# A tuned attention-and-MLP kernel: the first batch's second half is up-projected in seven products of quarters of 192 tokens

## The chip, the cores and the metric

The kernel runs on one core of a Trainium2 chip. The metric is the time of one execution on the device in microseconds. A core has a matrix engine (TensorE, in the profile PE, with PEld for its weight loads), VectorE (DVE), ScalarE (ACT), GpSimd (POOL), and SyncE (SP), which here only issues transfers. Each engine works through its own queue in order, and engines wait for one another by semaphores. TensorE writes its results to PSUM, from where VectorE or ScalarE takes them to the on-chip memory (SBUF).

## What is computed

Attention in which a query sees the keys of its own cluster only, then two matrix products with g = h - tanh(h) between them. Shapes: q, k, v (4 batches, 8 heads, 768 tokens, 64), centroids (8, 16, 64), w_in (512, 2048), w_out (2048, 512), all 32-bit floats in the kernel.

```python
q_assign = np.argmax(np.einsum('bhsd,hcd->bhsc', q_n, c_n), axis=-1)
k_assign = np.argmax(np.einsum('bhsd,hcd->bhsc', k_n, c_n), axis=-1)
mask = q_assign[:, :, :, None] == k_assign[:, :, None, :]
scores = np.where(mask, scale * np.matmul(q, k.transpose(0, 1, 3, 2)), -1000000000.0)
...
x = np.ascontiguousarray(attn_out.transpose(0, 2, 1, 3)).reshape(B * S, H * D)
h = x @ w_in
g = h - np.tanh(h)
return (g @ w_out).astype(np.float32)
```

## The kernel before

**Steps.** Attention is done for pairs of heads, four pairs a batch, and for a half of 384 query tokens at a time. One step of the outer loop (`for at, (n, half, s) in enumerate(steps)`) does a third of the keys for one pair and one half. The first batch does its first half for all four pairs (steps 0 to 11), then its second half (12 to 23); later batches take both halves of a pair together, 24 steps a batch. In each step TensorE gets the scores of the next step (`begin`, L451), and the products with the values (`value`, L505); ScalarE takes the exponentials (L473), VectorE selects by cluster code (`select`, L483), and GpSimd adds up the denominators (L496). After the last step of a pair the result lies in `xT[n][:, half]`, and a while later it is multiplied by the reciprocal of its denominator (`divide`, `scale`).

**The matrix products lag by one stage.** They are lists of items with a cost in planner's units, and each step takes the items that keep pace with an even share of the list. The first batch's first half is worked off in steps 12 to 23, its second half in steps 24 to 47, batches 1 and 2 in steps 48 to 71 and 72 to 95, and batch 3 at the end. An item calls `between()` once or twice, and each call emits a share of the step's other work (`todo`): selects first, then the stages of the next pairs' routing, then denominators, then weights to be rounded or factors to be made. So the order on every engine's queue follows from this list.

**Two forms of the products.** The first batch uses `plain_items`: 16 blocks of 128 of the 2048 inner columns, for each four chunks of 128 rows of w_in times 384 tokens (L676, tile `h`), tanh on ScalarE (L681) and the subtraction on VectorE (L683), then the products with w_out (L692, tile `o`). Later batches use `strassen_items`: inner columns, tokens and model columns are each cut in two, and seven products of quarters replace eight. Their left factors are sums of quarters of w_in and w_out, made once (`up_maker`, `down_maker`, L773), stored to device memory (L737, L756) and streamed back, one stream for each pair of blocks (`fetch_factors`, L795; tile `stream`, three buffers). Their right factors are differences of quarters of the attention output (`right_factors`, L832). `up_product` (L871, tile `pu`) does one of the seven, and each result is added on VectorE from PSUM (L859) or copied by ScalarE (L876); `shrink` then takes tanh (L864) and subtracts on GpSimd (L866). With three PSUM buffers (`ps_f`, shared by all small products), the fourth product from any one waits for nothing but the first's add.

**Memory.** The pool `first` holds what only the first batch needs (weights w_out, the tiles of g, rounding buffers `rawp`, and two pairs' transposed q and k in `turnp0`), `first_in` holds w_in. `open_stream` gives up w_in for the streams at step 39 and `open_late` gives up the rest at step 48. The factor sums use the three buffers of `rawp`, in which weights are rounded up to step 20. In steps 24 to 46, ten steps that are not at certain places in a pair (`light`) get a share of the makers' list.

Of the kernel before, what the change touches and what calls it, by code (L numbers as in the profile page):

```python
# [30 lines left out]
F32 = mybir.dt.float32  # L31
# [4 lines left out]
ALU = mybir.AluOpType  # L36
# [3 lines left out]
P = 128  # L40
# [18 lines left out]
def kernel(  # L59
# [119 lines left out]
    def fast():  # L179
# [439 lines left out]
        def spread_out(n: int, half: int):  # L619
            back = lists.pop((n, half))  # L620
            if joined(n):
                pool = late_pools.get("den", sump)
                dens[n, 1] = pool.tile([P, TB], F32, name="den")
                for i in range(2):
                    for h in range(2):
                        nc.sync.dma_start(
                            dens[n, i][h * D : h * D + D], back[i, h : h + 1].to_broadcast([D, TB])
                        )
                return
            for h in range(2):  # L630
# [34 lines left out]
        def plain_items(half: int):  # L665
# [39 lines left out]
            if half == 0:  # L705

                order = [(s, i) for i in range(NQ4) for s in range(2)] + order[2 * NQ4 :]
            return [(2.6, 1, lambda between, f=f: up(f, between)) for f in sequence] + [
                (3.4, 1, lambda between, s=s, i=i: project(s, i, between)) for s, i in order
            ]  # L710

# [74 lines left out]
        def fetch_factors(n: int):  # L786

            if n < (B - 1) * PER:
                i = n % PER
                t = streams[n] = late_pools["stream"].tile([P, HF, HM], F32, name="stream")  # L790
                if i < HF:
                    t = streams[n] = t.rearrange("p a b -> p (a b)")[:, 0 : 7 * CH * P].rearrange(
                        "p (c k f) -> p c k f", k=7, c=CH
                    )
                nc.sync.dma_start(t, up_factors[i] if i < HF else down_factors[i - HF])  # L795

        late_pools, diffs = {}, {}

        def open_stream():
            first_in.close()  # L800
            late_pools["stream"] = cx.enter_context(
                tc.tile_pool(name="stream_late", bufs=3, side="right", reuse_waits="tile")
            )
            late_pools["den"] = cx.enter_context(
                tc.tile_pool(name="den_late", bufs=1, side="right", reuse_waits="tile")
            )
            for n in range(2):
                fetch_factors(n)

        def open_late():  # L810
            first.close()
            for name, bufs in (
                ("diff", 1), ("u", 2), ("s", 2), ("th", 2), ("g", 1), ("left", 1), ("du", 1),
                ("c", 4), ("raw", 2),
            ):
# [4 lines left out]
            late_pools["S1"] = late_pools["left"].tile([P, HF, TB], F32, name="S1")  # L820

        def right_factors(b: int, c: int):

            if c == 0:
                diffs[b] = late_pools["diff"].tile([P, 3, CH, TB], F32, name="diff")
            d = diffs[b]
            x, y = xT[b * HP + c], xT[b * HP + CH + c]
# [6 lines left out]
        def strassen_items(b: int):  # L834
            base = (b - 1) * PER

            held = {}
            G, left1 = late_pools["G"], late_pools["S1"]

            def up_product(i: int, k_: int, between):  # L840
                which = PRODUCTS[k_]
                x = [xT[b * HP + c] for c in range(CD)]
                d = diffs[b]
                right = {
                    1: [x[c][:, 0] for c in range(CH)], 2: [x[CH + c][:, 0] for c in range(CH)],
                    3: [x[CH + c][:, 1] for c in range(CH)], 4: [d[:, 2, c] for c in range(CH)],
                    5: [d[:, 0, c] for c in range(CH)], 6: [d[:, 1, c] for c in range(CH)],
                    7: [x[c][:, 1] for c in range(CH)],
                }[which]
                if k_ == 0:  # L850
                    held[i] = (
                        late_pools["s"].tile([P, TB], F32, name="s"),
                        late_pools["u"].tile([P, 2, TB], F32, name="u"),
                    )
                s, u = held[i]
                g = G[:, i]

                def add(out, x, y):
                    nc.vector.tensor_tensor(out=out, in0=x, in1=y, op=ALU.add)  # L859

                def shrink(f: int, halves_=slice(0, 2)):
                    t = g[:, f, halves_]
                    th = late_pools["th"].tile([P, 2, TB], F32, name="th")[:, halves_]
                    nc.scalar.activation(out=th, in_=t, func=ACT.Tanh)  # L864
                    t, th = (x.rearrange("p a n -> p (a n)") for x in (t, th))
                    nc.gpsimd.tensor_tensor(out=t, in0=t, in1=th, op=ALU.subtract)  # L866

                ps = ps_f.tile([P, TB], F32, name="pu", tag="f")
                for c in range(CH):
                    for r in halves:  # L870
                        nc.tensor.matmul(  # L871
# [3 lines left out]
                if which == 1:  # L875
                    nc.scalar.copy(out=s, in_=ps)  # L876
                elif which == 2:
                    add(g[:, 0, 0], ps, s)
                    if i == HF - 1:
                        shrink(0, slice(0, 1))  # L880
                elif which == 6:
                    fetch_factors(base + i + 2)
                    add(u[:, 0], ps, s)
                elif which == 7:
                    add(u[:, 1], ps, u[:, 0])
                elif which == 4:
                    add(g[:, 1, 0], ps, u[:, 1])
                elif which == 5:
                    add(u[:, 0], ps, u[:, 0])
                    add(g[:, 1, 1], ps, u[:, 1])  # L890
                    shrink(1)
                else:
                    add(g[:, 0, 1], ps, u[:, 0])

                    shrink(0, slice(1 if i == HF - 1 else 0, 2))
                between()
                if k_ == len(PRODUCTS) - 1:

                    nc.gpsimd.tensor_tensor(out=left1[:, i], in0=g[:, 0, 1], in1=g[:, 1, 1], op=ALU.add)
                    nc.gpsimd.tensor_tensor(  # L900
                        out=g[:, 0, 1], in0=g[:, 0, 0], in1=g[:, 0, 1], op=ALU.subtract
                    )
                    streams.pop(base + i)

            us = {}

            def down_product(k_: int, j: int, between):
# [49 lines left out]
                between()  # L957


            return [  # L960
                (1.3, 1, lambda between, i=i, k_=k_: up_product(i, k_, between))
                for i in range(HF) for k_ in range(len(PRODUCTS))
            ] + [
                (3.4, 2, lambda between, k_=k_, j=j: down_product(k_, j, between))
                for k_ in range(len(PRODUCTS)) for j in range(HCH)
            ]
# [136 lines left out]
        for at, (n, half, s) in enumerate(steps):  # L1103
            b, p = pairs[n]
            following = steps[at + 1] if at + 1 < len(steps) else None
            if at == 4 * HALF:
                open_late()
            if at == 4 * HALF - 9:
                open_stream()
            if at in fills:  # L1110
                fill, over = fills[at][0](), fills[at][1]
                whole, spent, since = sum(it[0] for it in fill), 0.0, at
            if at == 2 * HALF:
                makers = [it for i in range(2) for it in up_maker(i)]
                makers += [it for i in range(2) for it in down_maker(i)]
            now = []
            part = (at - since + 1) / over
            while fill and (spent + fill[0][0] / 2 <= whole * part or part == 1):
# [86 lines left out]
            listed = []  # L1205

            light = [i for i in range(at, 4 * HALF - 2) if i % 3 and i % 6 != 1]
            if makers and at in light:
                share = -(-len(makers) // len(light))
                todo += makers[:share]  # L1210
                del makers[:share]
# [24 lines left out]
            it()  # L1236
        right_factors(B - 1, CH - 1)
        tail = strassen_items(B - 1)

        PRS = len(PRODUCTS)  # L1240
        tail = tail[:2] + tail[PRS : PRS + 2] + tail[2:PRS] + tail[PRS + 2 :]
        for it in tail[:2]:
            it[2](lambda: None)

# [215 lines left out]
```

## Time and profile before

Median of three runs: 982.78 us (982.29 to 982.94). The profiled execution has a span of 981.3 us.

| engine | busy, us | instructions |
|---|---|---|
| TensorE, matmuls | 972.3 | 6456 |
| TensorE, weight loads | 461.1 | 6456 |
| VectorE | 534.5 | 1010 |
| ScalarE | 316.6 | 484 |
| GpSimd | 498.8 | 347 |

Where the stages lie, by the chain of waits: up-products of the first half start at 79.8 us, its projection at 142.4, the up-products of the second half at 205.9, its projection at 290.1, the later batches' up-products at 374.7, 607.5 and 830.3. The first batch's steps 20, 21, 22 and 23 begin their scores at 159.9, 170.3, 180.5 and 190.3 us.

How to read it: a group's line gives line of code, engine, operation, output and inputs, shapes and count; behind the bar the busy time in us and the mean of one in ns; behind the next the idle time before them and what ended it. The chain of waits is followed back from the last instruction; its pieces in order of time have start, length, what, and the number of instructions. A window's line gives each engine's busy time in a stretch, the clock as a share of full speed, the share of the transfer engines' time and the GB/s. Matmuls overlap at their ends, so their busy times are a little longer than their spacing.

### The profile page before, as it was taken

The page shows a single profiled execution, that of the slowest core. Times are in us where ns is not written, and L with a number is a line of the kernel's source. Part 1 is how long each engine was busy: PE and PEld are TensorE (multiplying, and loading weights), DVE is VectorE, ACT ScalarE, POOL GpSimd, SP SyncE. Part 2 cuts the span into 40 slices and gives each one's busy share as a digit, 9 for nine tenths or more (in the row PEclk, how much of TensorE's full clock was granted, in tenths as well). Part 3 has the DMA queues.
Part 4 walks back from the last instruction along what each step waited for, and adds up shares of the span by engine and source line. Part 5 has one row for each costly group of instructions (what it writes and reads, how often), then busy time and mean ns, then how long its engine had stood idle before and what let it go on. Part 6 is the DMA issues. An engine that isn't in the chain of part 4 may idle for free.

```text
span 981.3 us, 16550 instructions
## 1 busy us (share of the span) xinstructions
PE 972.3 (99%) x6456; PEld 461.1 (47%) x6456; DVE 534.5 (54%) x1010; ACT 316.6 (32%) x484; POOL 498.8 (51%) x347
## 2 busy tenths in 40 slices
PE   9999999999999999999999999999999999999997
PEld 5433443344443334444455555444455555444664
DVE  6458656447566577647655457655754436543011
ACT  5586554233332333233422222333242121222000
POOL 1026334445445454677686345666688445466600
PEclk9999999999999999999999999999999999999999
DMA  7664452024665633463544646345343132233221
GB/s 201 185 192 142 147 143 94 30 73 132 156 204 166 173 116 110 148 195 99 186 151 158 189 136 201 110 151 149 123 159 135 62 118 95 83 113 129 104 103 35
DMA packets 113385, 132.47 MB, mean 135 GB/s; under 512 B 60388, under 2 KB 93076, under 8 KB 110612
## 3 DMA queue, kind: packets, MB, share of 16 engines
q1 hardware_dynamic: 106916, 109.81, 36.5%
q0 software_dynamic: 6240, 21.50, 6.3%
q8 instruction: 53, 0.87, 0.4%
q14 instruction: 32, 0.26, 0.1%
q10 hardware_dynamic: 144, 0.03, 0.0%
HBM read 110.14 MB, written 21.17 MB: 134 GB/s over the span
## 4 chain that ended last, share of the span: by engine, by line
PE 97%; DVE 1%; DMA 0%; issue 0%; SPq 0%; ACT 0%; DVEq 0%
PE pd L922 22%; PE pu L871 22%; PE sc L451 14%; PE av L505 14%; PE o L692 8%; PE h L676 8%; PE pt L332 2%; PE sim L351 1%; PE den L520 1%; PE warm L302 1%; PE den L566 1%; PE den L539 1%; PE pr L364 1%; DVE e L483 1%; DMA row<-q_codes 0%; PE pq L396 0%
## 5 line engine op out<-in xcount | busy, mean ns | idle before, releaser
L496 POOL TENSOR_TENSOR sum<-sum,e 128x768 f32<-128x768 f32 x112 | 207.2, 1850 | 98.0 <-DVE e L483 92.1
L483 DVE SCALAR_TENSOR_TENSOR e<-row,code,sc 128x384 f32<-128x384 bf16 x336 | 186.2, 607 | 104.2 <-ACT sc L473 89.9
L473 ACT ACTIVATE sc<-sc 128x768 f32<-128x768 f32 x168 | 125.9, 792 | 215.8 <-PE sc L451 206.4
L922 PE MATMUL pd<-stream,G 128*64 128x256 f32 x1728 | 191.5, 379 | 0.0
L922 PEld LDWEIGHTS pd<-stream,G 128*64 128x64 f32 x1728 | 123.7, 137 | 67.0 <-issue 7.7
L451 PE MATMUL sc<-t,t 64*128 64x384 f32 x768 | 150.2, 509 | 0.4 <-ACT e L473 0.3
L505 PE MATMUL av<-e,vals 128*64 128x384 f32 x768 | 145.6, 498 | 0.4 <-DVE e L483 0.4
L871 PE MATMUL pu<-xT,stream 128*64 128x384 f32 x768 | 134.9, 488 | 0.7 <-DVE top L372 0.7
L866 POOL TENSOR_TENSOR G<-G,th 128x768 f32<-128x768 f32 (+1 forms) x51 | 87.3, 1723 | 93.9 <-ACT th L864 93.9
L871 PE MATMUL pu<-diff,stream 128*64 128x384 f32 x576 | 102.3, 488 | 0.0
L451 PEld LDWEIGHTS sc<-t,t 64*128 64x128 f32 x768 | 65.8, 186 | 75.0 <-issue 40.8
L492 POOL TENSOR_TENSOR sum<-e 128x768 f32<-128x768 f32 x28 | 55.5, 1983 | 77.9 <-DVE e L483 42.2
L871 PEld LDWEIGHTS pu<-xT,stream 128*64 128x64 f32 x768 | 54.1, 137 | 69.6 <-issue 61.9
L864 ACT ACTIVATE th<-G 128x768 f32<-128x768 f32 (+1 forms) x51 | 40.9, 806 | 141.2 <-DVE G L859 141.2
L692 PE MATMUL o<-w_out,g 128*64 128x512 f32 x384 | 86.4, 594 | 0.0
L505 PEld LDWEIGHTS av<-e,vals 128*64 128x64 f32 x768 | 47.5, 136 | 82.5 <-issue 79.7
L676 PE MATMUL h<-xT,w_in 128*64 128x384 f32 x512 | 86.3, 487 | 0.0
L871 PEld LDWEIGHTS pu<-diff,stream 128*64 128x64 f32 x576 | 40.4, 137 | 51.0 <-issue 44.7
L859 DVE TENSOR_TENSOR G<-pu,u 128x384 f32<-128x384 f32 x72 | 39.8, 553 | 43.5 <-PE pu L871 43.5
L676 PEld LDWEIGHTS h<-xT,w_in 128*64 128x64 f32 x512 | 36.4, 137 | 46.2 <-issue 45.1
L933 DVE SCALAR_TENSOR_TENSOR c<-pd,du 128x256 f32<-128x256 f32 x36 | 15.2, 421 | 67.0 <-PE pd L922 67.0
L692 PEld LDWEIGHTS o<-w_out,g 128*64 128x64 f32 x384 | 27.0, 137 | 50.1 <-issue 49.4
(131 smaller groups left out, 828.9 us busy)
## 6 DMA issues: line engine op xcount, KB each, us to landing
stream<-up_factors SPq DMA_DIRECT2D x24, 896.0 KB
stream<-down_factors SPq DMA_DIRECT2D x21, 1024.0 KB
raw<-in_moe_w_in_dram POOLq DMA_DIRECT2D x16, 512.0 KB, 4.7
raw<-in_moe_w_out_dram POOLq DMA_DIRECT2D x16, 512.0 KB, 3.9
again<-in_moe_w_in_dram SPq DMA_DIRECT2D x32, 256.0 KB
again<-in_moe_w_out_dram SPq DMA_DIRECT2D x32, 256.0 KB
x<-in_q_dram SPq DMA_DIRECT2D x32, 192.0 KB
x<-in_k_dram SPq DMA_DIRECT2D x32, 192.0 KB
```

The source lines that it names most:

```text
L451: nc.tensor.matmul(sc[i][:, h, 0:TB], lhsT=turned[n, 1][r].rearrange("p a n -> p (a n)")[:, j * P : (j + 1) * P], rhs=turned[n, 0][r, half ...
L473: nc.scalar.activation(out=out, in_=sc[i][:, :, 0:TB], func=ACT.Exp, scale=SCALE)
L483: nc.vector.scalar_tensor_tensor(out=e[:, h], in0=rows[n, half][:, h], scalar=codes[n][:, 1, j // HCH, h, j % HCH : j % HCH + 1], in1=sc[: ...
L492: nc.gpsimd.tensor_tensor(out=s, in0=pair[0], in1=pair[1], op=ALU.add)
L496: nc.gpsimd.tensor_tensor(out=s, in0=s, in1=pair[i], op=ALU.add)
L505: nc.tensor.matmul(avs[n, half][h * D : h * D + D], lhsT=vals[n][:, h, j], rhs=e[i][:, h], start=(j == 0), stop=(j == NCH - 1),)
L676: nc.tensor.matmul(h[r], lhsT=w_in[i][:, c, o * P : (o + 1) * P][:, r], rhs=xT[c][:, half], start=(c == 0), stop=(c == CD - 1),)
L692: nc.tensor.matmul(acc[sub][r], lhsT=gs[f % HF][:, f // HF, sub * P : (sub + 1) * P][:, r], rhs=w_out[f // FQ][:, f % FQ], start=(f == seq ...
L864: nc.scalar.activation(out=th, in_=t, func=ACT.Tanh)
L866: nc.gpsimd.tensor_tensor(out=t, in0=t, in1=th, op=ALU.subtract)
L871: nc.tensor.matmul(ps[r], lhsT=streams[base + i][:, c, k_, r], rhs=right[c], start=(c == 0), stop=(c == CH - 1),)
L922: nc.tensor.matmul(ps[r], lhsT=left(i)[:, r], rhs=t[:, i], start=(i == 0), stop=(i == HF - 1))
```

## The change

The up-projection of the first batch's second half takes the seven-product form, with its 384 tokens cut into two quarters of 192. It replaces 16 blocks of plain products by 8 x 7 products of half the rows, to do an eighth less multiplication. For this the up factors have to exist earlier: they are made in steps 20 to 22, at the end of the first half's stage, the space of w_in is given up at step 23, and the first two streams are fetched there. The up factors are then streamed once more than before (eight more streams). The projection of that half stays as it was.

The seven-product code becomes `up_items`, shared by both uses, with functions for where a quarter of g lies, how it is shrunk, and what follows a finished block. Tiles for the first batch's use come from pools that live at that time: partial sums in `turnp0`, right factors in a pool of their own. The late buffer for denominators moves: before step 48 it is now a tile of `turnp0`. The order that starts two blocks' first two products ahead of the third, until now only at the end of the kernel, is a function used twice.

```diff
@@ plain_items
-            return [(2.6, 1, lambda between, f=f: up(f, between)) for f in sequence] + [
+            ups = [(2.6, 1, lambda between, f=f: up(f, between)) for f in sequence]
+            if half == 1:
+                ups = half_up_items(gs)
+            return ups + [
                 (3.4, 1, lambda between, s=s, i=i: project(s, i, between)) for s, i in order
@@ spread_out
-                pool = late_pools.get("den", sump)
-                dens[n, 1] = pool.tile([P, TB], F32, name="den")
+                if "den" in late_pools:
+                    dens[n, 1] = late_pools["den"].tile([P, TB], F32, name="den")
+                else:
+                    dens[n, 1] = turnp0.tile([P, 2, TB], F32, name="t0")[:, 0]
@@ fetch_factors, open_stream
-                i = n % PER
+                i = n + HF if n < 0 else n % PER
...
+            half_pools["diff"] = mid.enter_context(
+                tc.tile_pool(name="diff_mid", bufs=1, side="right", reuse_waits="tile")
             )
             for n in range(2):
-                fetch_factors(n)
+                fetch_factors(n - HF)
@@ up_items (from strassen_items)
+            width = TB if b else TB // 2
...
-                ps = ps_f.tile([P, TB], F32, name="pu", tag="f")
+                ps = ps_f.tile([P, TB], F32, name="pu", tag="f")[:, 0:width]
...
+        def start_without(items):
+            n = len(PRODUCTS)
+            return items[:2] + items[n : n + 2] + items[2:n] + items[n + 2 :]
...
+            def shrink(i: int, f: int, parts):
+                cols = slice(parts.start * W, parts.stop * W)
+                t = gs[i][:, f, cols]
+                th = thp.tile([P, TB], F32, name="th")[:, cols]
+                nc.scalar.activation(out=th, in_=t, func=ACT.Tanh)
+                nc.gpsimd.tensor_tensor(out=t, in0=t, in1=th, op=ALU.subtract)
+
+            return start_without(up_items(0, -HF, quarter, shrink, lambda i: None))
@@ the loop over steps
-            if at == 4 * HALF - 9:
+            if at == 2 * HALF - 1:
                 open_stream()
...
+            if at == 2 * HALF - 4:
+                makers = [it for i in range(2) for it in up_maker(i)]
             if at == 2 * HALF:
-                makers = [it for i in range(2) for it in up_maker(i)]
-                makers += [it for i in range(2) for it in down_maker(i)]
+                makers = [it for i in range(2) for it in down_maker(i)]
...
             light = [i for i in range(at, 4 * HALF - 2) if i % 3 and i % 6 != 1]
+            if at < 2 * HALF - 1:
+                light = list(range(at, 2 * HALF - 1))
...
-            if at in fills and "raw" in late_pools:
+            if at == 2 * HALF or (at in fills and "raw" in late_pools):
                 for c in range(CH - 1 if at > 4 * HALF else 0, CH):
                     right_factors(b - 1, c)
```

More of the change, by code (lines that the diff above doesn't have):

```diff
@@ L795, in fetch_factors @@
                 nc.sync.dma_start(t, up_factors[i] if i < HF else down_factors[i - HF])
-        late_pools, diffs = {}, {}
+        late_pools, half_pools, diffs = {}, {}, {}
+        mid = ExitStack()
         def open_stream():
@@ L803, in open_stream @@
             )
-            late_pools["den"] = cx.enter_context(
-                tc.tile_pool(name="den_late", bufs=1, side="right", reuse_waits="tile")
+            half_pools["diff"] = mid.enter_context(
+                tc.tile_pool(name="diff_mid", bufs=1, side="right", reuse_waits="tile")
             )
             for n in range(2):
-                fetch_factors(n)
+                fetch_factors(n - HF)
         def open_late():
             first.close()
+            mid.close()
             for name, bufs in (
                 ("diff", 1), ("u", 2), ("s", 2), ("th", 2), ("g", 1), ("left", 1), ("du", 1),
-                ("c", 4), ("raw", 2),
+                ("c", 4), ("raw", 2), ("den", 1),
             ):
@@ L820, in open_late, with columns @@
             late_pools["S1"] = late_pools["left"].tile([P, HF, TB], F32, name="S1")
+        def columns(b: int, c: int):
+            return xT[b * HP + c] if b else xT[c][:, 1].rearrange("p (a n) -> p a n", a=2)
         def right_factors(b: int, c: int):
             if c == 0:
-                diffs[b] = late_pools["diff"].tile([P, 3, CH, TB], F32, name="diff")
+                diffs[b] = (
+                    late_pools["diff"].tile([P, 3, CH, TB], F32, name="diff")
+                    if b else half_pools["diff"].tile([P, 3, CH, TB // 2], F32, name="diff")
+                )
             d = diffs[b]
-            x, y = xT[b * HP + c], xT[b * HP + CH + c]
+            x, y = columns(b, c), columns(b, CH + c)
             for out, u, w in (
@@ L832, in right_factors, with up_items @@
                 nc.vector.tensor_tensor(out=out, in0=u, in1=w, op=ALU.subtract)
-        def strassen_items(b: int):
-            base = (b - 1) * PER
+        def up_items(b: int, base: int, quarter, shrink, done):
             held = {}
-            G, left1 = late_pools["G"], late_pools["S1"]
+            width = TB if b else TB // 2
             def up_product(i: int, k_: int, between):
                 which = PRODUCTS[k_]
[L842 to L849, printed above, removed]
-                if k_ == 0:
[L851 to L854, printed above, removed]
+                x = [columns(b, c) for c in range(CD)]
+                d = diffs[b] if which in (4, 5, 6) else None
+                if which in (4, 5, 6):
+                    right = [d[:, {5: 0, 6: 1, 4: 2}[which], c] for c in range(CH)]
+                else:
+                    rows_, half = {1: (0, 0), 2: (CH, 0), 3: (CH, 1), 7: (0, 1)}[which]
+                    right = [x[rows_ + c][:, half] for c in range(CH)]
+                if k_ == 0:
+                    if b:
+                        held[i] = (
+                            late_pools["s"].tile([P, width], F32, name="s"),
+                            late_pools["u"].tile([P, 2, width], F32, name="u"),
+                        )
+                    else:
+                        t = turnp0.tile([P, 2, TB], F32, name="t1")
+                        held[i] = t[:, 0, 0:width], t[:, 1].rearrange("p (a n) -> p a n", a=2)
@@ L855, in up_product @@
                 s, u = held[i]
-                g = G[:, i]
                 def add(out, x, y):
                     nc.vector.tensor_tensor(out=out, in0=x, in1=y, op=ALU.add)
[L861 to L866, printed above, removed]
@@ L877, in up_product @@
                 elif which == 2:
-                    add(g[:, 0, 0], ps, s)
+                    add(quarter(i, 0, 0), ps, s)
                     if i == HF - 1:
-                        shrink(0, slice(0, 1))
+                        shrink(i, 0, slice(0, 1))
                 elif which == 6:
@@ L886, in up_product @@
                 elif which == 4:
-                    add(g[:, 1, 0], ps, u[:, 1])
+                    add(quarter(i, 1, 0), ps, u[:, 1])
                 elif which == 5:
                     add(u[:, 0], ps, u[:, 0])
-                    add(g[:, 1, 1], ps, u[:, 1])
-                    shrink(1)
-                else:
-                    add(g[:, 0, 1], ps, u[:, 0])
-                    shrink(0, slice(1 if i == HF - 1 else 0, 2))
+                    add(quarter(i, 1, 1), ps, u[:, 1])
+                    shrink(i, 1, slice(0, 2))
+                else:
+                    add(quarter(i, 0, 1), ps, u[:, 0])
+                    shrink(i, 0, slice(1 if i == HF - 1 else 0, 2))
@@ L896, in up_product @@
                 between()
                 if k_ == len(PRODUCTS) - 1:
[L899 to L902, printed above, removed]
+                    done(i)
                     streams.pop(base + i)
+            return [
+                (1.3 * width / TB, 1, lambda between, i=i, k_=k_: up_product(i, k_, between))
+                for i in range(HF) for k_ in range(len(PRODUCTS))
+            ]
@@ new lines, in start_without, with half_up_items, quarter @@
+        def start_without(items):
+            n = len(PRODUCTS)
+            return items[:2] + items[n : n + 2] + items[2:n] + items[n + 2 :]
+        def half_up_items(gs):
+            W = TB // 2
+            def quarter(i: int, f: int, t: int):
+                if i not in gs:
+                    gs[i] = gp.tile([P, 2, TB], F32, name="g")
+                return gs[i][:, f, t * W : (t + 1) * W]
+            def shrink(i: int, f: int, parts):
[5 more added lines that the diff above has]
+            return start_without(up_items(0, -HF, quarter, shrink, lambda i: None))
@@ new lines, in strassen_items, with shrink, done @@
+        def strassen_items(b: int):
+            base = (b - 1) * PER
+            G, left1 = late_pools["G"], late_pools["S1"]
+            def shrink(i: int, f: int, parts):
+                t = G[:, i, f, parts]
+                th = late_pools["th"].tile([P, 2, TB], F32, name="th")[:, parts]
+                nc.scalar.activation(out=th, in_=t, func=ACT.Tanh)
+                t, th = (x.rearrange("p a n -> p (a n)") for x in (t, th))
+                nc.gpsimd.tensor_tensor(out=t, in0=t, in1=th, op=ALU.subtract)
+            def done(i: int):
+                g = G[:, i]
+                nc.gpsimd.tensor_tensor(out=left1[:, i], in0=g[:, 0, 1], in1=g[:, 1, 1], op=ALU.add)
+                nc.gpsimd.tensor_tensor(
+                    out=g[:, 0, 1], in0=g[:, 0, 0], in1=g[:, 0, 1], op=ALU.subtract
+                )
@@ L957, in down_product @@
                 between()
[L960 to L963, printed above, removed]
+            return up_items(b, base, lambda i, f, t: G[:, i, f, t], shrink, done) + [
                 (3.4, 2, lambda between, k_=k_, j=j: down_product(k_, j, between))
@@ L1238, in fast @@
         tail = strassen_items(B - 1)
-        PRS = len(PRODUCTS)
-        tail = tail[:2] + tail[PRS : PRS + 2] + tail[2:PRS] + tail[PRS + 2 :]
+        tail = start_without(tail)
         for it in tail[:2]:
```

## The prediction

> **What bounds the kernel now.** I read the page's engine totals first, then TensorE's waits, then the chain of waits with its pieces in order of time, then the groups by shape and the windows by stage.
>
> The page's first lines, and every wait of TensorE:
>
> ```profile
> span 981.3 us, 16550 instructions
> PE 972.3 (99%) x6456; PEld 461.1 (47%) x6456; DVE 534.5 (54%) x1010; ACT 316.6 (32%) x484; POOL 498.8 (51%) x347
> ```
>
> ```profile
> PE warm L302 <- DVE inverses L231: 1.3, 1, 1.3
> PE pu L871 <- DVE top L372: 0.7, 2, 0.3
> PE av L505 <- DVE e L483: 0.4, 1, 0.4
> PE sc L451 <- ACT e L473: 0.3, 1, 0.3
> PE sim L351 <- ACT t L339: 0.2, 1, 0.2
> ```
>
> TensorE waits 2.9 us in the whole program, and never between 206 and 374 us, where the changed stage lies. So the time is TensorE's work, and a change to that work moves the end one to one, unless it brings a wait. I leave the clock out: it is 1.00 in every window I asked for.
>
> Since busy times of pipelined matmuls overlap at their ends, I take prices from the chain of waits (start, length, what, number of instructions):
>
> ```profile
> 231.35 5.16 PE h L676 x32
> ...
> 392.93 6.45 PE pu L871 x40
> ...
> 491.44 6.91 PE pd L922 x64
> ```
>
> and from the same view of an early stretch:
>
> ```profile
> 29.83 0.78 PE den L520 x8
> ...
> 32.58 0.33 PE sc L462 x4
> ...
> 38.60 1.46 PE pt L332 x12
> ```
>
> Per instruction: h and pu at 384 columns 161.25 ns, pd at 256 columns 108.0 ns. pu has the same price as h although it changes its accumulator after 8 instructions and h after 16, so a new group costs nothing. Instructions run as pairs, one for each half of the output rows: 322.5 and 216 ns a pair, which is 2 x columns / 2.4 + 2.5 ns both times.
>
> **What the Trainium skill says.** "TensorE: Matmul & The Clock Gate", section "Wait — 56ns, not 53.3ns?": consecutive matmuls at full clock are N / 2.4 ns apart plus a fixed 2.5 ns or so. The pairs here agree to 0.2 ns, counted as 2N columns. The same page, "LDWEIGHTS (loading the stationary operand)", prices a weight load by its columns over 1.2, 53 ns for 64; the trace's loads last 137 ns, two together, so I use 137. "TensorEngine Tiling (Array Packing)", "PSUM Bottleneck", warns that shorter TensorE work doesn't make the emptying of PSUM shorter; no wait before shows it, and it is my first rival. "DMA: Bandwidth & Descriptors", "Specifications", wants 512 bytes or more for line rate; a factor store here moves runs of 128 four-byte values, exactly 512, and the stretch in which six of them ran reached 265 GB/s.
>
> **The change, part by part.**
>
> *Up-projection of the second half (steps 24 to 35).* Removed: 16 blocks x 4 row chunks x 2 halves, two instructions each, 256 instructions x 161.25 ns = 41.3 us. Added: 8 blocks x 7 products x 2 chunks x 2 halves x 2 = 448 instructions of 192 columns. By the line that fits 256 and 384 columns, a pair is 384 / 2.4 + 2.5 = 162.5 ns, one instruction 81.25 ns, the sum 36.4 us. Gain 4.9 us, all on the path. The least this can be is 80 ns (no fixed part): 35.8 us. The most: nothing in the trace sustains less than 97.5 ns for 8 instructions in a row (den); at that price the sum is 43.7 us. Break-even is 41.3 / 448 = 92.2 ns. I take 81.25: a pair of loads (137 ns) fits beside a pair of matmuls (162.5 ns), the four masks of line 462 ran at 81 ns each with a load apiece, and a transpose of line 332, which loads 128 columns (as many as our two loads together), repeats every 1.46 / 12 = 122 ns, below our 162.5.
>
> *VectorE.* By shape:
>
> ```profile
> L859 DVE TENSOR_TENSOR G<-pu,u 128x384 f32<-128x384 f32 x72 | 39.8, 553 | 43.5 <-PE pu L871 43.5
> ...
> L683 DVE TENSOR_TENSOR g<-h,th 128x384 f32<-128x384 f32 x32 | 17.6, 551 | 26.4 <-ACT th L681 26.3
> ...
> L933 DVE SCALAR_TENSOR_TENSOR c<-pd,du 128x256 f32<-128x256 f32 x36 | 15.2, 421 | 67.0 <-PE pd L922 67.0
> ```
>
> The line through 256 (421 ns) and 384 (553 ns) gives 355 ns for 192. Gone from the up stage: 16 subtractions, 8.8 us, and the up factors' eight sums, 9.8 us (they move ahead). New: 8 adds per block, 64 x 355 = 22.7 us, and about three of the down factors' sums that now come earlier, 4.2 us. The windows, with the columns PE, PEld, DVE, ACT and POOL busy, clock, DMA share and GB/s (stage changed; a later up stage of the product form; where factors are made now; the fullest DMA stretch):
>
> ```profile
> 206.00:290.00 84.00, 84.00 (x512) 36.12 (x510) 54.22 (x87) 32.49 (x53) 39.37 (x20) 1.00 0.46 131
> 374.00:490.00 116.00, 115.66 (x704) 49.11 (x702) 71.89 (x142) 41.12 (x61) 78.81 (x50) 1.00 0.46 150
> 158.00:190.00 32.00, 32.00 (x159) 11.11 (x155) 18.70 (x32) 10.55 (x16) 14.72 (x11) 1.00 0.20 63
> ```
>
> ```profile
> 246.00:254.00 8.00, 8.00 (x52) 3.35 (x46) 4.20 (x8) 3.97 (x6) 3.79 (x3) 1.00 1.06 265
> ```
>
> VectorE: 54.2 - 8.8 - 9.8 + 22.7 + 4.2 = 62.5 us in 84.0 - 4.9 = 79.1 us, 79%, against 62% in the later stage of this form, which loses 0.3 us of TensorE. ScalarE swaps 16 tanh for 16 tanh and 8 short copies (about 0.34 us each, below the 0.38 of 256 columns): +3 us of a 39% load. GpSimd gets 16 subtractions of 128x384 at 1.00 us: 55 of 79 us. None becomes the bound.
>
> *The wait it makes likelier.* A product lasts 8 x 81.25 = 0.65 us and there are three PSUM buffers, so its add must have ended within 1.3 us of it, else the third product after it waits. Behind the add on VectorE stand the next block's two selects (1.13 us), and TensorE's value products wait for those. Add after select is 1.13 + 0.36 = 1.5 us: up to 0.2 us of stall where a select stands between two early products of a step. A step of this stage gets 77.2 / 24 = 3.2 of the planner's units, five products at 0.65. A select falls between the first two in the six steps whose list is longest (those with a factor sum), and the scores and values at the head of each step (1.49 + 1.44 us without any product) let VectorE catch up. 0.2 x 6 = 1.2 us at most if all hit, 0 if none. I take 0.5.
>
> *Up factors made in steps 20 to 22.* Eight sums of 1.22 us, 9.8 us of VectorE, go to a stretch (158 to 190) with 18.7 busy of 32: 28.5 of 32. Selects stand ahead of them in each step and the next selects' results are needed some 8 us later, so they hide. A sum needs one of three buffers, whose store must have landed: stores are 28 x 256 KB = 7.3 MB, 28 us at 265 GB/s in the 30.4 us between the scores at 159.87 and 190.27. They are issued from 168 on, when the last weights are rounded, and I estimate the last landing near 195. The same stores leave the steps from 24 on.
>
> *First two factor streams at step 23.* They wait on the sync queue for all stores; behind them stand the loads of batch 1's third pair (now 198.1), needed a step later than the streams. 0.9 MB each at 265 GB/s is 3.5 us: they land near 199 and 203. TensorE wants them at 205.9, the first h, and 1.3 us after. Slack 4 to 7 us: no cost.
>
> *Right factors of the half:* 8 subtractions x 355 = 2.8 us, on a VectorE idle from 198.7 to 206.2. *Pools, the denominators' new place, the reordering of the tail into a function:* no instruction of the later batches changes. Nothing.
>
> Sum: 982.8 - 4.9 + 0.5 = 978.4 us.
>
> **Rivals.** (1) VectorE sets the pace in the up stage: the product took half the time, its add only went from 553 to 355 ns. For it: 79% is above any product stage here, and adds and selects interleave. Against: the later stage's zero waits, and 0.65 us of TensorE against 0.36 us. If every one of the 11 steps loses 0.3 us: 982.8 - 4.9 + 3.3 = 981.2, about no change. (2) The factors come late: 7.3 MB in one burst. At 183 GB/s (the window 230 to 238 us, with the same stores at their present pace) the stores take 40 us, from 169 to 209; a stream of 3.5 us and about 1 us to land brings the first product to 213.7, 7.8 us late: 982.8 - 4.9 + 0.5 + 7.8 = 986.2, slower. Against: DMA is at 0.20 there, and 265 GB/s was seen. (3) Short matmuls don't reach their price, because loads or issue take 97.5 ns each: 43.7 us instead of 41.3, 982.8 + 2.4 = 985.2, slower. Against: the 81 ns of line 462, though only four long.
>
> **How the numbers follow.** My forecast 0.72, rival 1 0.10, rival 2 0.10, rival 3 0.08. The bottom of the range is the 80 ns price and no stall, 982.8 - 5.5 = 977.3. The top is rival 1 with room for its own spread, 982.0; the two slower rivals, 0.18, stay out. Faster by over 0.2% means below 980.8: my case and a part of rival 1, 0.78; within 0.2%: most of rival 1 and a mild rival 2, 0.09; slower 0.13.
>
> **What would show it.** Runs of eight 192-column products at 0.65 us in the chain; 448 new pu instructions and 256 fewer h; TensorE's waits on VectorE in the up stage below 1 us in sum; the stage near 79 us; no TensorE gap at the first product; the last factor store before about 196 us. Wrong would be: a pu price over 92 ns, waits of pu on a VectorE add or on a stream, or value products waiting for selects in steps 21 to 24.

## The result, and the profile after

The changed kernel takes 989.43 us (median of six, 988.37 to 990.38), the kernel before 982.86 (median of six, 982.29 to 983.37). The ratio is 1.0067, 95% interval 1.0054 to 1.0080: 6.6 us slower, where 4.4 us faster was forecast. The profiled execution is the fastest of the six, 988.37 us.

The page's first lines after:

```profile
span 986.5 us, 17050 instructions
PE 970.7 (98%) x6648; PEld 473.8 (48%) x6648; DVE 550.3 (56%) x1058; ACT 319.2 (32%) x493; POOL 515.4 (52%) x364
```

The matrix work did shrink. The span grew all the same, so TensorE waits now. Its waits between 206 and 290 us, where it waited for nothing before (who waited for whom: us in total, times, longest):

```profile
PE sc L451 <- DVE e L483: 2.5, 4, 0.7
PE pt L332 <- ACT th L935: 1.9, 1, 1.9
PE pu L881 <- DVE g L876: 0.8, 2, 0.4
PE pt L332 <- ACT den L571: 0.5, 1, 0.5
PE pr L364 <- DVE g L876: 0.2, 1, 0.2
```

These sum to 5.9 us; one more wait of scores on a select, 0.7 us, lies at 306 us. That is less than the loss, because a wait in this view counts only from the end of the matmul before: the record of a score matmul is 483 ns long, while the next pair of matmuls usually starts 320 ns after it, and the pair after a wait needs 0.42 us instead of 0.32. So a wait of the scores hides some 0.2 to 0.3 us more. Measured from the first product of the stage to the first of batch 1 (steps 24 to 47), the stretch was 168.8 us (205.9 to 374.7) and is 174.4 us (205.3 to 379.8). By the matmul prices alone it should have become 163.9, so 10.5 us are lost. Sorted by what TensorE does, from each operation's first start to the next operation's, so that a wait counts with the operation ahead of it:

| | before, us | after, us | difference |
|---|---|---|---|
| h, then products of 192 | 42.6 | 40.2 | -2.4 |
| scores | 34.3 | 38.5 | +4.2 |
| values | 32.6 | 33.4 | +0.8 |
| den (denominators) and pt (transposes) | 9.6 | 12.5 | +2.9 |
| the rest | 48.3 | 48.5 | +0.2 |

(The last operation's own length is left out of both columns, so that they add up to 167.3 and 173.0.) The products fell by 2.4 us instead of 4.9; 2.0 us of this difference lie in four of their 15 runs, three of which hold a wait of the list or end in one. Where nothing waits, the products keep the price: in the chain, 40 instructions of 192 columns without a wait take 3.25 us, 81.25 ns each.

```profile
234.25 3.25 PE pu L881 x40
```

How the new wait comes about is seen at the head of step 25. TensorE's timeline:

```profile
207.91 0.82 PE L881 MATMUL pu<-diff,stream 128*64 128x192 f32 x8
208.66 0.92 PE L451 MATMUL sc<-t,t 64*128 64x384 f32 x4
210.27 0.92 PE L451 MATMUL sc<-t,t 64*128 64x384 f32 x4 [0.70 <-DVE e L483]
```

and VectorE's at the same time:

```profile
206.90 0.36 DVE L876 TENSOR_TENSOR g<-pu,t 128x192 f32<-128x192 f32 x1 [5.52 <-PE pu L881]
207.18 1.13 DVE L483 SCALAR_TENSOR_TENSOR e<-row,code,sc 128x384 f32<-128x384 bf16 x2
208.55 0.36 DVE L876 TENSOR_TENSOR g<-pu,t 128x192 f32<-128x192 f32 x1 [0.25 <-issue]
208.83 0.35 DVE L876 TENSOR_TENSOR t<-pu,t 128x192 f32<-128x192 f32 x1
209.09 1.13 DVE L483 SCALAR_TENSOR_TENSOR e<-row,code,sc 128x384 f32<-128x384 bf16 x2
```

ScalarE finished the exponentials of the two score tiles of this step at 205.6 and 206.3:

```profile
204.78 1.50 ACT L473 ACTIVATE sc<-sc 128x768 f32<-128x768 f32 x2 [0.40 <-PE sc L451]
```

VectorE had been idle for 5.5 us when it started its first add at 206.9, and for the last 1.3 of these the first select could have run: it is queued behind that add, which needs the second product that TensorE makes after the step's scores and values. The second select (209.09 to 210.22) is queued behind the fifth product's add, and the second score tile of the next step needs the PSUM buffer which that select empties. There are two such buffers (`ps_s`), so TensorE waits until 210.27. In the kernel before, a block's share of the selects was emitted ahead of that block's subtraction, and no such chain of adds stood in front of them.

Two more lines for steps of the prediction. The window of the up stage, and the sync queue's timeline at its beginning:

```profile
206.00:290.00 84.00, 77.99 (x673) 47.08 (x670) 60.91 (x122) 32.38 (x58) 55.12 (x37) 1.00 0.54 170
```

```profile
192.82 3.32 SPq L743 DMA_DIRECT2D up_factors<-made  x4
196.19 1.70 SPq L801 DMA_DIRECT2D stream<-up_factors  x2
```

VectorE has 60.9 us of work in 84 us, about what was worked out. The last store is issued before 196.2, the first streams right behind it, and the first product starts at 205.3 without a wait.

### The profile page after: what moved, and what is told of

Its sections match the earlier page's. It is cut to its first block, busy times and chain, and to the rows that moved or that the text cites. A ratio compares the mean times of both kernels' runs of the same rounds, so it can differ in the third digit from the quotient of the medians.

```text
span 986.5 us, 17050 instructions
## 1 busy us (share of the span) xinstructions
PE 970.7 (98%) x6648; PEld 473.8 (48%) x6648; DVE 550.3 (56%) x1058; ACT 319.2 (32%) x493; POOL 515.4 (52%) x364
## 4 chain that ended last, share of the span: by engine, by line
PE 93%; DVE 4%; DMA 1%; issue 1%; ACT 0%; SPq 0%; DVEq 0%; ACTq 0%
PE pu L881 23%; PE pd L977 22%; PE av L505 13%; PE sc L451 13%; PE o L695 8%; PE h L679 4%; PE pt L332 2%; DVE e L483 2%; PE sim L351 1%; PE den L520 1%; PE warm L302 1%; PE den L539 1%; DMA down_factors<-w_out 1%; PE den L566 1%; PE pr L364 1%
## 5 line engine op out<-in xcount | busy, mean ns | idle before, releaser
L881 PE MATMUL pu<-xT,stream 128*64 128x384 f32 (+1 forms) x1024 | 159.9, 448 | 1.1 <-DVE top L372 0.7
L881 PE MATMUL pu<-diff,stream 128*64 128x384 f32 (+1 forms) x768 | 121.1, 448 | 0.4 <-DVE g L876 0.3
L881 PEld LDWEIGHTS pu<-xT,stream 128*64 128x64 f32 x1024 | 71.8, 137 | 76.9 <-issue 65.7
L881 PEld LDWEIGHTS pu<-diff,stream 128*64 128x64 f32 x768 | 53.8, 137 | 55.4 <-issue 46.3
L988 DVE SCALAR_TENSOR_TENSOR du<-pd,du 128x256 f32<-128x256 f32 x27 | 11.3, 420 | 60.4 <-PE pd L977 60.4
L679 PE MATMUL h<-xT,w_in 128*64 128x384 f32 x256 | 42.9, 487 | 0.0
```

The lines of the kernel that those rows point to most:

```text
L679: nc.tensor.matmul(h[r], lhsT=w_in[i][:, c, o * P : (o + 1) * P][:, r], rhs=xT[c][:, half], start=(c == 0), stop=(c == CD - 1),)
L881: nc.tensor.matmul(ps[r], lhsT=streams[base + i][:, c, k_, r], rhs=right[c], start=(c == 0), stop=(c == CH - 1),)
```

## The experiments

Theory A says that the order on VectorE's queue is at fault: selects behind late adds. Rival B says that VectorE simply has too much to do; rival C that GpSimd slows it down. Each run has its own measurement of the kernel before beside it; behind a ratio stands its 95% interval.

**1. Selects first.** In steps 24 to 35, and with them the denominators' product where it stands between the two:

```diff
+            if following and 2 * HALF <= at < 3 * HALF:
+                both = 3 if half == 1 and s == NS - 1 and joined(n) else 2
+                for it in todo[:both]:
+                    it()
+                del todo[:both]
             for it in now:
                 it[2](between)
```

> Changed kernel, but in steps 24 to 35 the two selects of the next step are emitted ahead of the step's products. Theory A (order): the scores of the next step need PSUM buffers that the selects empty, and the selects stand on VectorE behind adds of products that TensorE makes late in the step; with selects first the waits of sc and pt on VectorE (3.2 and 2.4 us, with their drains about 6.5 us) go: 980 to 984 us. Rival B (load): VectorE simply has too much work in the stage, slowed further by GpSimd; the order changes nothing: 988 to 990 us.

Measured: 983.86 us (983.07 to 984.90, 12 runs), before 983.39; ratio 1.0007 (0.9998 to 1.0016). 5.6 of the 6.6 us are gone (by the ratios 5.9) with the same instructions in another order. No score and no transpose waits between 206 and 290 us; products do, instead:

```profile
PE pu L881 <- DVE t L876: 1.4, 2, 0.8
PE pu L881 <- DVE g L876: 1.4, 1, 1.4
```

**2. The down factors' sums out of the stage**, order as in the changed kernel:

```diff
-            light = [i for i in range(at, 4 * HALF - 2) if i % 3 and i % 6 != 1]
+            light = [i for i in range(max(at, 3 * HALF), 4 * HALF - 2) if i % 3 and i % 6 != 1]
```

> Changed kernel, but the down factors' sums (five or six of 1.2 to 2.6 us on VectorE between steps 26 and 35) are all made from step 38 on. Order of the rest as in the changed kernel. Theory A (order): only what the sums delayed behind them goes, 986 to 988 us, and the gaps between the two score tiles of a step stay near 0.7 us. Rival B (load): 9 to 10 us of VectorE leave the stage, most of the loss goes: 981 to 984 us.

Measured: 992.05 us (991.04 to 992.09, 4 runs), ratio 1.0085 (1.0068 to 1.0102). Both expectations missed, and rival B by far: with less for VectorE to do, the kernel is no faster than the changed one, and if anything slower (1.0085 against 1.0067, with intervals that overlap). The list explains it. `between()` spreads the list evenly over a step's slots. With five slots, a list of two selects and three makers' items puts the selects behind the first and second product, a list of the two selects alone puts them behind the third and fifth. Taking the sums away moved the selects later, and the scores waited more often:

```profile
PE sc L451 <- DVE e L483: 5.4, 10, 0.9
PE pt L332 <- ACT t L339: 1.1, 1, 1.1
PE av L505 <- DVE e L483: 0.4, 1, 0.4
```

**3. Both edits.**

> Both edits: selects first in steps 24 to 35, and the down factors' sums from step 38 on. Theory A: as the first run less at most 2 us, 978 to 982 us, near the 977.9 that the matmul prices alone give. Rival B: as the run with the sums later, 981 to 984 us.

Measured: 982.26 us (981.72 to 983.19, 20 runs), before 983.39, ratio 0.9989 (0.9982 to 0.9996): better than both kernels, and than the kernel before by little. This is just outside what theory A gave and inside rival B's range, so the number doesn't tell them apart; runs 1 and 4, which change only the order, do. Once selects don't depend on the list, the sums' leaving helps, by 1.6 us: the amount of work counts too, but less than the order.

**4. Selects last**, in steps that don't end a pair's half:

```diff
+            if following and 2 * HALF <= at < 3 * HALF and s < NS - 1:
+                todo = todo[2:] + todo[:2]
             slots = max(sum(it[1] for it in now), 1)
```

> Changed kernel, but in those steps from 24 to 35 that do not end a pair's half the two selects go to the end of the step's list, behind sums and routing. The work is the same. Theory A: the waits of the score tiles grow, 992 to 997 us. Rival B: same work, 988 to 990 us.

Measured: 1001.59 us (999.60 to 1004.67, 4 runs), ratio 1.0195 (1.0170 to 1.0219). The same work, 12 us slower than the changed kernel. Theory A holds in sign and was too small in size:

```profile
PE sc L451 <- DVE e L483: 14.1, 15, 2.1
```

**5. Fewer products in a step.** Run 3, with the planner's cost of a product at 0.8 instead of 0.65, by `((1.3 if b else 1.6) * width / TB, ...)`.

> Selects first and sums later, and the planner's cost of a 192-column product raised from 0.65 to 0.8, so that a step gets four or five products, not five, and every later step gets a projection item. Theory A with its remainder (adds of five products crowd behind selects and routing, two stalls of pu of 0.6 and 0.8 us and their drains, and one step at 306 us without an item that waits 0.7 us for its selects): 979.5 to 981.5 us. If what remains is a cost of the short products themselves: as the third run, 982 us.

Measured: 984.25 us (983.65 to 986.01, 21 runs), ratio 1.0012 (1.0006 to 1.0019). Missed. The last products slipped into step 36, which the edit of the selects doesn't reach, and the product waits stayed:

```profile
PE sc L451 <- DVE e L483: 1.6, 2, 1.2
PE pu L881 <- DVE g L876: 1.6, 2, 0.8
PE pu L881 <- DVE t L876: 0.7, 1, 0.7
```

**6. The early sums alone.** The kernel before, with the up factors made in steps 20 to 22; no product of quarters, no early streams.

> Kernel before, with the up factors made in steps 20 to 22 and nothing else of the change (no product of quarters, no earlier streams). If the burst of 28 stores and eight sums hides, as predicted: 982.5 to 983.7 us, as before. If the early sums are a part of the loss: 984 to 987 us.

Measured: 983.30 us (12 runs), before 983.22, ratio 0.9999 (0.9990 to 1.0008). No cost. VectorE's busy time between 158 and 190 us went from 18.7 to 28.2 us, and TensorE's line has no gap:

```profile
158.00:190.00 32.00, 32.00 (x159) 11.27 (x157) 28.21 (x39) 10.39 (x16) 14.34 (x11) 1.00 0.69 204
```

**7. Less GpSimd.** The changed kernel without the subtraction of the tanh in the stage:

```diff
-                th = thp.tile([P, TB], F32, name="th")[:, cols]
-                nc.scalar.activation(out=th, in_=t, func=ACT.Tanh)
-                nc.gpsimd.tensor_tensor(out=t, in0=t, in1=th, op=ALU.subtract)
+                nc.scalar.activation(out=t, in_=t, func=ACT.Tanh)
```

> Changed kernel that leaves out the subtraction on GpSimd in the 192-column stage (g becomes tanh(h) there), to take 16 us off GpSimd. Theory A (order): VectorE's sums and routing no longer stretch to 2 us and more where GpSimd runs beside them, but the selects still stand behind late adds: 986 to 989 us. Rival C (GpSimd slowing VectorE is the cause): 980 to 984 us.

Measured: 987.30 us (986.99 to 987.56, 4 runs), ratio 1.0043 (1.0027 to 1.0059). 17 us less of GpSimd save 2.1 us (by the ratios 2.4, with intervals that just overlap). The waits of the scores are what they were; the transposes' longest, which the profile puts down to ScalarE, fell from 1.9 to 0.9 us, those of the products from 0.8 to 0.3.

```profile
206.00:290.00 84.00, 79.36 (x686) 48.11 (x686) 59.77 (x122) 33.94 (x60) 37.73 (x20) 1.00 0.58 173
```

```profile
PE sc L451 <- DVE e L483: 2.5, 4, 0.7
PE pt L332 <- ACT g L934: 0.9, 1, 0.9
```

So rival C is a part of the loss, about a fifth of the 10.5 us, and not its main cause.

**8. Selects first in the kernel before**, as a control.

> Kernel before, with the selects ahead of the step's items in steps 24 to 35, as a control: TensorE waits for no select there, so nothing is to be gained: 982.6 to 983.8 us. If the order of selects alone gave the third run its gain: 981.5 to 982.5 us.

Measured: 983.63 us (12 runs), before 983.22, ratio 1.0004 (0.9996 to 1.0013). The order gains nothing where nothing waits.

**9. One select first.** As run 3, but in each step with a quarter product the second select goes behind the second product's add:

```diff
+            second = []
+            if following and any(it[0] < 1.0 for it in now):
+                both = 3 if half == 1 and s == NS - 1 and joined(n) else 2
+                for it in todo[: both - 1]:
+                    it()
+                second = todo[both - 1 : both]
+                del todo[:both]
...
                 i = next(place)
+                if second and i >= min(1, slots - 1):
+                    second.pop()()
```

> As the third run (sums later), but in every step with a quarter product only the first select goes ahead of the products, and the second goes behind the second product's add. Theory A, sharpened: VectorE's queue has two deadlines in a step, the selects' by the next step's scores and the first adds' by the fourth product (three PSUM buffers); both selects first misses the second where scores come late or routing stands ahead. The two pu waits of 0.6 and 0.8 us go, the wait at 306 us stays: 980 to 981.5 us. If those waits have another cause: as the third run, 982.3 us.

Measured: 982.38 us (13 runs), before 982.98, ratio 0.9993 (0.9985 to 1.0002). The product waits are gone, as foreseen. The gain isn't there, and the time is that of run 3, as the other expectation had it, for another reason: the product that ends a pair's denominators (den, emitted ahead of the products) now comes before GpSimd has its sums, since these follow the second select. Eight den matmuls take 1.54 us there, against 0.85 in a step without a wait, and the second transpose waits 0.9 us.

```profile
279.14 1.54 PE L566 MATMUL den<-sum,ones 128*32 128x384 f32 x8
...
283.82 0.88 PE L332 MATMUL pt<-ident,x 128*128 128x128 f32 x6 [0.89 <-ACT t L339]
```

**10. Run 9 with cost 0.8.**

> The ninth run with the planner's cost of a product at 0.8, as in the fifth. Theory A: the fifth run lost 3.9 us in five waits, three of adds behind selects and two in a step behind the edit's reach; all go, and no step is without an item at 306 us: 978.5 to 980.5 us. If four to five products a step cost something of themselves: 982 us or more.

Measured: 983.29 us (13 runs), ratio 1.0005 (0.9996 to 1.0013). Missed. The number lies in the range of the other expectation, that four or five products a step cost something of themselves; but waits of den (1.1 us), of scores (1.1) and of a product (0.7) remain, and run 12, with hardly more products a step, has no such cost.

**11. Run 9 with den behind the second product, and cost 0.73**, so that products and projections take twelve steps each.

> The ninth run, with two more edits: the denominators' product that ends a pair (den, 1.0 us late there behind GpSimd's sums) goes with the second select behind the second product, and the planner's cost of a product is 0.73, so that products and projections take twelve steps each and no step is left without an item. Theory A: the waits of den, pt and of sc at 306 us go, the products keep their 85 to 86 ns: 979 to 981 us. If each edit only moves the wait to another product: 982 us.

Measured: 981.23 us (median of 19; one execution took 2010.93 us, for which nothing here gives a cause), before 982.87, ratio 0.9983 (0.9976 to 0.9990). This is just above what theory A gave; one wait of den, 0.6 us, is left.

**12. By the step.** Both selects first, except in steps whose scores come late (values first) or that follow a routing, where the second goes behind the second product; sums later; cost 0.73:

```diff
+                late_scores = values_first or 2 in ready.get(at - 1, {})
+                first_few = both - 1 if late_scores and both == 2 else both
+                for it in todo[:first_few]:
+                    it()
+                second = todo[first_few:both]
```

> Selects both ahead of the products as in the third run, except in steps whose scores come late (values first) or follow a routing, where the second goes behind the second product; sums later; cost 0.73. Theory A: the third run's two pu waits and its wait at 306 us go, and nothing comes in their place: 979 to 981 us. If each edit only moves the wait: 982 us.

Measured: 979.54 us (979.29 to 979.94, 6 runs), before 982.87, ratio 0.9964 (0.9952 to 0.9977): 3.3 us faster than before and 9.9 faster than the changed kernel, with the same matrix work, and as theory A had it. Between 206 and 290 us TensorE has one wait:

```profile
PE pu L881 <- DVE t L876: 0.2, 1, 0.2
```

Steps 24 to 47 take 165.1 us (206.1 to 371.2), against the 163.9 that the prices give. VectorE's and GpSimd's columns in the window of the up stage are 54.3 and 55.0 us, so GpSimd is as busy as in the changed kernel:

```profile
206.00:290.00 84.00, 83.81 (x722) 50.77 (x720) 54.31 (x121) 35.30 (x63) 55.02 (x38) 1.00 0.49 142
```

Of the 10.5 us lost in steps 24 to 47, the order alone (run 1, 169.3 us) brings back 5.1, the sums' leaving (run 3, 167.7) 1.7 more, and the finer order with the new cost (run 12) 2.6 more. Run 12 changes these last two together.

## Why the prediction was wrong

**The gain on TensorE was right.** 81.25 ns an instruction was forecast and measured, run 12 gets 3.7 of the 4.9 us in steps 24 to 47, and rival 3 (97.5 ns) is out.

**The step that failed is "The wait it makes likelier".** It put 0.5 us where 10.5 us were lost, half of which the order alone brings back (run 1), and said "1.2 us at most if all hit". Two things were wrong in it.

The first is the deadline. It said that "TensorE's value products wait for those" selects, and let scores and values at the head of a step (1.49 and 1.44 us) be time for VectorE to catch up. But the next scores write into the two PSUM buffers that the selects empty, so the first select is due at the head of the step, and the second 0.75 us after it, not after the scores. The kernel's text shows it (`ps_s` with two buffers, `begin` ahead of `value`); the prediction counted only the three buffers of the products. The waits of the scores after (2.5 us up to 290), and their 14.1 us in run 4, show it on the chip.

The second is where the select stands. The prediction feared the steps with the longest lists, where a select falls between the first two products. It is the other way round: with a short list the selects stand behind the third and fifth product. Run 2 made the lists shorter and the scores' waits longer (5.4 us instead of 2.5), run 1 took the selects out of the list and got 5.6 us back.

Den and pt (2.9 us) have the same root as far as the runs show: pt writes into the same two buffers, and its waits of 1.9 and 0.5 us, which the profile puts down to ScalarE, each ended 0.1 us after a select did; both are gone in run 1, which moves only the selects and the denominators' product between them. The fear for the products' own three buffers was right in kind: when selects come first, the products wait (2.8 us in run 1, 1.4 in run 3), and run 9 removes that, run 12 all but 0.2 us.

**The sum of VectorE's work came out near by luck, and proves nothing.** 62.5 us were worked out for 79.1, and 60.9 were measured in 84. A block has seven adds, not the eight that were counted: 56 in the trace, 19.6 us instead of 22.7. Against this, the factor sums grew by 7.0 us instead of 4.2, and two sums of the routing (L375) by 2.6 us that were not counted; the rest is mostly that neighbouring records overlap by 7.8 us in the window instead of 4.9, which the busy time counts once. Whatever the sum, VectorE had time to spare, and a select whose input was ready stood still behind an add. With much the same work on VectorE (59.9 us in the same window) and another order, run 1 is 5.6 us faster.

**Rival 1 named the right engine and the wrong reason.** It held that VectorE sets the pace by the amount of its work, and gave 981.2 for 0.3 us in each of 11 steps. The measured loss is about 1 us a step; with the same work, half of it goes when the selects come first (run 1), and it doubles, to 21.0 us in steps 24 to 47, when they come last (run 4).

**Hidden as forecast:** the early sums (run 6: 0.9999), the stores (last one issued before 196.2; landing was put at 195) and the first stream. Rival 2 is out. The third stream was issued at 204.8 only, behind loads of keys whose issue took 5.3 us, and still no product waited for it.

**GpSimd** had the work that was worked out (55.1 us), **ScalarE** 3 us less (32.4 against 35.5), and neither became the bound. What GpSimd's new work does to the others was left out: 2.1 us by run 7.

What is left open: why run 12 stays 1.2 us above the prices in steps 24 to 47. A run of products costs about 0.1 us beyond its price in the kernel before too, and run 12 has 15 of them instead of 12, some 0.3 us; another 0.7 us lie in one run of products (from 277.4 us), in which the one wait on VectorE stands. No run takes these apart.

## What to carry to other kernels

When a product gets shorter, look not at the sum of the work of the engine that empties it but at its queue: for every instruction in it, which buffer does it free, when does TensorE want that buffer, and which instruction ahead of it waits for something that TensorE makes late. Put work whose input is ready early, and whose buffer is wanted at the head of the next step, ahead of work whose input comes late. A list that is spread evenly over slots is a hidden order: taking items from it moves the others.

## What the hardware showed unexpectedly

VectorE's operations with both inputs in SBUF can get almost four times as long when GpSimd works beside them. The same line with the same shape, between its shortest and longest (a line's instructions: duration min/median/max), after:

```profile
L375 DVE TENSOR_TENSOR top<-top,down x16: 557/828/2109, 13.4 to 744.4; 128x384 f32<-128x384 f32 x16
...
L779 DVE TENSOR_TENSOR made<-w_out x2: 2115/2350/2585, 224.4 to 284.3; 128x1024 f32<-128x1024 f32 x2
```

The sums of the second line took 1.21 us in the kernel before, both times. The selects, which read scores from PSUM, lie between 598 and 615 ns in the stage. "SBUF — State Buffer", section "Who interferes with whom", in the Trainium skill, says so: a VectorE instruction with two SBUF inputs contends with a GpSimd instruction that reads SBUF, one with at most one such input doesn't, outside VectorE's two-port modes. The trace agrees, and adds that it isn't every such meeting: in the changed kernel the instructions of L375 and L779 without a GpSimd instruction beside them took 557 to 559 ns and 1.21 to 1.23 us, and of those beside one some took as little, others up to 2.11 and 2.83 us.

The prediction priced the sums undisturbed, at 1.2 us. Between 206 and 290 us, five of them and two routing sums (L375) took 13.2 us, where 7.2 would be the undisturbed time. Only a fifth of these 6 us is due to tanh's subtraction on GpSimd: without it (run 7) they still took 12.0 us, beside GpSimd's sums for the denominators.
